# The second half of v begins with tokens 1024 to 1535, read from tiles still on chip; loads of heads and gate are spread over more units

## The chip, the cores and the metric

The kernel runs on one core of one Trainium2 chip. The metric is the time of one execution on the device, in microseconds; for the kernel before it is the median of three runs. A profile is one further execution of the same program, taken with the hardware profiler, and has a time of its own.

## The reference

Two attention blocks of 32 heads work on the same x (2048 tokens, 1024 columns): A is linear attention, B is softmax attention, and a gate g, one number per token, mixes their outputs.

```python
x = A_x                                              # 1 x 2048 x 1024, fp32
g = _sigmoid((x * gate_w).sum(-1, keepdims=True))
# A: q, k, v = x @ A_wqkv; phi(t) = where(t > 0, t + 1, exp(t)) + 1e-6
#    kv = phi(k)^T v, z = sum(phi(k)); o = phi(q) kv / (phi(q) z + 1e-6); a = o @ A_wo
# B: q, k, v = x @ B_wqkv; p = softmax(q k^T * Dh ** -0.5); o = p v; b = o @ B_wo
return g * a + (1 - g) * b
```

## The kernel before

fp32 products are made of three fp32r products: each operand is split into a high and a low part, and `three` (lines 148 to 157) issues high by high, high by low and low by high into one PSUM bank. A matmul has a stationary part of 128x128 and a moving part of 128x512.

**Opening (lines 526 to 671).** x stands on chip as tiles of the program's `big` set, in two passes: J = 0 holds tokens 0 to 1023, J = 1 tokens 1024 to 2047. In a pass, `X11`, `X21`, `X12`, `X22` hold the split x: `X` with row l + 1 and column jj + 1 holds the k-blocks k with k % 2 = l and the 512 tokens 2J + jj. Each piece is a pair of `big` tiles, high and low. `PLACE` (line 307) says which: for J = 1 it puts X11 in (4, 5), T4 (and X12) in (8, 9), X21 in (10, 11), X22 in (12, 13), T1 in (0, 1), T2 in (2, 3), T3 in (6, 7). `v_pass` makes the first 512 columns of v of block B; then sixteen `quad`s make q and k of B by a Strassen-like scheme of seven products each, in the order X11, X21, X22, T1, T2, T3, T4. The split x of all tokens is written to DRAM (`xs`) by `spill`. q and k go to DRAM as `qk`, v as `v`.

**The last quad** of J = 1 runs beside `leave()` (lines 674 to 688), one step of it between products: it splits the weights of the second half of v into `big` 16 to 19 and loads the first three halves of x for the next stage.

**The linear stage, `linear()` (line 926).** It runs over units. A unit is a kind, a chunk of columns and one tile of 128 tokens: first sixteen units "v" (the second 512 columns of v of block B, tokens 0 to 15 in order of tiles), then "kv", "q" and "o" for block A. A unit makes 24 matmuls, eight k-steps of three. Its stationary x comes from DRAM: `load_half(m)` (line 761) loads half m, that is four k-blocks of unit m // 2, high and low, 256 KB each, into `xh_t[m % 3]`, three buffers, two of them in `big` 4. The load of half m + 3 is issued right after the matmuls that read half m. In the sixteen "v" units other things are issued at fixed k-steps: `first`, fourteen loads of q, k and v of heads 0 and 1 (`load_q`, `load_k`, `load_v`, 64 KB per piece, 192 KB for the rest of a q), and the steps of `gate()` (line 487): each loads one tile of x (512 KB, two buffers) and has VectorE multiply the tile before it with the gate's weights and sum it (line 495). So the load of an x waits for the product that last read its buffer.

**Beside it.** `maxima()` makes the score products of a head (line 1123), and VectorE takes the maximum of each row (line 1128); during the "v" units a rule lets it begin after six units, with eight or nine products in each of the units after that. `rows(h)` turns the maxima (PE, line 1140) and writes them to `big` as `mh` and `ml`. From unit 16 on, `heads_()` makes the exponentials and the products with v. A planner (lines 1589 to 1693) puts the streams in order while the program is built, by modelled costs; what it issues is fixed then. PE executes its instructions in this order.

**Queues.** All loads and stores here go through `dma` (line 166) and are issued by the SP engine, in the program's order: an issue that has to wait for its buffer holds up all that stand behind it. The exception are the folds of the heads' sums, which POOL issues.

**The turn to kv.** In units 14 and 15 the weights of the kv units are loaded (`load_w`, line 715) and split by ACT and VectorE (lines 728 and 730) into the places of v's weights, as these come free.

In the "q" units, `queries` turns a result; a "q" unit waits until the one three units before it has been turned. `keys_alone(n)` issues what is left of the products of keys up to unit n.

Of the kernel before, what the change touches and what calls it, by code (L numbers as in the profile page):

```python
# [19 lines left out]
P = 128  # L20
# [27 lines left out]
def kernel(  # L48
# [23 lines left out]
    HK = NK // 2  # L72
    NT = S // P
# [230 lines left out]

    KH = NK // 2
    NPAIR = NJ // 2
    PLACE = [(4, 5), (8, 9), (10, 11), (12, 13), (0, 1), (2, 3), (6, 7)]
    PRODUCTS = ["X11", "X21", "X22", "T1", "T2", "T3", "T4"]
    PLACES = [dict(zip(PRODUCTS, PLACE)), dict(zip(["X11", "T4", "X21", "X22", "T1", "T2", "T3"], PLACE))]
    for side in PLACES:  # L310
# [22 lines left out]
    def xpiece(J, name, p, i):  # L333
        return side_x(J, name, p)[:, i * C:(i + 1) * C]

    def xname(jj, l):
        return "X%d%d" % (l + 1, jj + 1)
# [16 lines left out]
    def v_out(c, t, ps, va):  # L354
        nc.scalar.copy(va, ps)  # L355
        dma(v_d[c][:, t, :], va)
# [316 lines left out]

    def leave():

        load_half(0)
        load_half(1)
        split_v1(raw_a[2], 2)
        split_v1(raw_a[3], 3)
        yield  # L680
        xh_t[2] = sb.tile([P, 2 * HK * P], F32R, name="xh")
        load_half(2)
        split_v1(raw_a[0], 0)
        split_v1(raw_a[1], 1)
        yield
        for k in range(KH, NK):
            split_v1(raw_b[k - KH], k)
            yield
# [67 lines left out]
    def xstat_lin(n, k, p):  # L756

        o = (p * HK + k % HK) * P
        return xh_t[(2 * n + k // HK) % 3][:, o:o + P]

    def load_half(m):

        if m >= 2 * len(units):
            return
        i, t = units[m // 2]
        ks = slice(m % 2 * HK, (m % 2 + 1) * HK)
        for p, src in enumerate(oA_d if chunks[i][0] == "o" else xs):
            o = p * HK * P
            dma(f32(xh_t[m % 3][:, o:o + HK * P].rearrange("p (k c) -> p k c", c=P)), src[t][:, ks])
        xp_ready[m] = T["sp"] + 3.2  # L770
# [155 lines left out]
    def linear():  # L926
# [9 lines left out]
        for n, (i, t) in enumerate(units):  # L936
            kind, c = chunks[i]
            follow = chunks[i + 1] if i + 1 < len(chunks) else None
            lag = 2 if kind == "v" else 0

            def renew(k):

                mark = Later(None, 0.0, 0.0, 0, None)
                w_left[k][:] = [mark]
                next_w.append((follow, k, mark, nc.vector if kind == "v" else nc.gpsimd))
                pump_w(kind == "v")

            yield bank_at
            b = take()
            ps = bank[b]  # L950
            T["pe"] = max(T["pe"], free[b])
            lin_kind[0] = kind
            if (kind, c, t) in (("q", 1, 2), ("q", 1, 8), ("o", 0, 2), ("o", 0, 8)):
                load_mix()
            for k in range(NK):
                yield lambda: ended(w_left[k], w_ready[k], xp_ready.get(2 * n + k // HK, 0.0))
                need(w_left[k])
                stat = [xstat_lin(n, k, p) for p in range(2)]
                for m, _ in enumerate(three(ps, stat, (wpart(k, 0), wpart(k, 1)), k)):
                    lin_pe(1.0)  # L960
                    if m < 2:
                        yield always
                store_mix()
                if kind == "v":
                    if first and (k == 1 or k == 5 and t):
                        first.popleft()()
                    if t > TPC and k in (3, 7):
                        next(gates, None)
                if k % HK == HK - 1:
                    load_half(2 * n + k // HK + 3)  # L970
                if k == 0 and n + 7 == len(units) and not o_main[0]:
                    load_o(0)
                if k == 1 and n + 1 == len(units):
                    assert finished[0] >= H - 2
                    need(pr_left[extra_pr[2]])
                    xo_t[0] = big_tile(PR[extra_pr[2]], F32R)
                    split_o(0, slice(0, NK - 1))
                if k == NK // 2 and n + 1 == len(units) and over["head"]:
                    split_o(1, slice(0, NK - 1))
                if k == NK - 1:  # L980
                    yield from extra
                if follow and follow[0] == "o":
                    if t == NT - 1:
                        w_left[k].clear()
                        yield lambda: 0.0 if mixed.count((k // HK, follow[1])) == 8 * HK else None
                        load_wa(follow[1], k)
                    continue
                if follow and t == NT - 2 and k == 0:
                    yield lambda: None if mix_here or stores else 0.0
                if follow and t == NT - 2 and k < min(LEAD_W, NK):  # L990
                    coming_w.append(load_w(*follow, k, LEAD_W + 1))
                if follow and t == NT - 1 and k >= lag:
                    renew(k - lag)
            extra = iter(())
            e, r = mid[3 + n % 3], mid[6]
            if kind == "v":
                give(b, use("act", 0.5, T["pe"] + LATENCY["pe"]))
                v_out(c, t, ps, mid[11 - n % 2])
            elif kind == "kv":
                va = mid[7][:, (n % 2) * HC:(n % 2 + 1) * HC]  # L1000
                yield from keys_alone(n - 2)
                nc.scalar.copy(va, ps[:, HC:])
                use("act", 0.28, T["pe"] + LATENCY["pe"])
                end = phi(ps, e, HC)

                def more(end, c=c, t=t, e=e, ps=ps):
                    pk = e[:, :HC]
                    nc.vector.scalar_tensor_tensor(pk, pk, 1.0, ps[:, :HC], op0=ALU.min, op1=ALU.add)
                    z_end[c % 2] = use("pool", 0.69, end)
                    if t == 0:  # L1010
                        nc.gpsimd.tensor_copy(zsum[c % 2], pk)
                    else:
                        nc.gpsimd.tensor_add(zsum[c % 2], zsum[c % 2], pk)

                todo = [defer(more, end, 0.34)]
                give(b, 0.0, todo)
                keys(n, c, t, e, va, todo)
                if t == NT - 1:
                    extra = keysum(c)
            elif kind == "q":  # L1020
                yield lambda: None if n - 3 not in turned and chunks[units[n - 3][0]][0] == "q" else 0.0
                end = phi(ps, e, C)
                d = dn[n % 2]

                def sums(_, e=e, ps=ps):
                    nc.vector.scalar_tensor_tensor(ps, e, 1.0, ps, op0=ALU.min, op1=ALU.add)

                def scaled(_, c=c, ps=ps, r=r):
                    nc.vector.tensor_mul(r, ps, zrep[:, c * C:(c + 1) * C])

                last = []

                def dens(end, r=r, d=d, last=last):
                    nc.vector.tensor_reduce(d, r.rearrange("p (h d) -> p h d", d=DH), AX.X, ALU.add)
                    nc.scalar.add(d, d, eps)
                    last[0].at = use("act", 0.2, end)

                def divide(_, t=t, e=e, ps=ps, d=d):
                    nc.vector.reciprocal(d, d)
                    nc.vector.scalar_tensor_tensor(  # L1040
                        e.rearrange("p (h d) -> p h d", d=DH), ps.rearrange("p (h d) -> p h d", d=DH),
                        g_sb[:, t:t + 1], d.unsqueeze(2).to_broadcast([P, C // DH, DH]),
                        op0=ALU.mult, op1=ALU.mult)

                todo = chain(((sums, 0.63), (scaled, 0.63), (dens, 0.63), (divide, 0.9)), end)
                last.append(todo[-1])
                give(b, 0.0, todo)
                tasks.append((lambda todo=todo: None if kv_todo else both(ended(todo + o_left), o_free[(len(turned) + 1) % 2], bank_at()),
                              lambda n=n, c=c, t=t, e=e, todo=todo: queries(n, c, t, e, todo)))
            else:  # L1050
                res = mid[(7, 10)[n % 2]]
                give(b, use("act", 0.5, T["pe"] + LATENCY["pe"]))
                nc.scalar.copy(res, ps)
                dma(ra_d[t][:, c * C:(c + 1) * C], res)
            if follow and follow[0] != "o" and t == NT - 1:
                for k in range(NK - lag, NK):
                    renew(k)
# [661 lines left out]
```

## Time and profile before

| | us |
|---|---|
| median of three runs | 2843.2 |
| lowest, highest | 2840.29, 2846.19 |
| the profiled execution, its time | 2843.68 |
| its span, first to last instruction | 2841.9 |
| PE busy | 2823.3 |
| DVE busy | 2229.5 |
| POOL busy | 1909.1 |
| ACT busy | 1596.6 |

The span is what the profile covers; the time holds some 1.8 us more around it. In the profile an engine is named PE (matmuls), PEld (weight loads, beside PE), DVE (VectorE), ACT (ScalarE), POOL (GpSimd), SP (the queue of DMA issues). A timeline row gives the start, the duration, engine and line, the operation, and what was written from what; brackets give the idle time of the engine before it and what ended it. A windows row gives a stretch, its length, the busy time and instructions of each engine, the mean granted clock of PE, the share of the DMA engines that was busy, and GB/s. Matmuls overlap, and each row of one shows some 0.39 us, so the distance of two starts says more than a duration.

### The profile page before, as it was taken

Reading aid. Unit: us, or ns where it says so; the run is one execution under the profiler, and the core shown is the slowest. Engines: PE = TensorE matmul, PEld = TensorE weight load, DVE = VectorE, ACT = ScalarE, POOL = GpSimd, SP = SyncE. Lnnn points to the kernel's source line nnn. Section 1 sums busy time; section 2 is a strip of 40 time slices with the busy share of each in tenths; the row PEclk is TensorE's granted clock in tenths of the full one; section 3 lists DMA queues with packets and bytes.
Section 4 is the critical chain, followed back from the end, with each engine's and each line's share of the span. In section 5 each row is a group of like instructions: output and inputs, shape, how many; then the busy total and the mean of one; then the engine's idle time right before and its main releaser. Section 6 shows DMA issues by size and latency. Waiting matters only on the chain.

```text
span 2841.9 us, 46542 instructions
## 1 busy us (share of the span) xinstructions
PE 2823.3 (99%) x15944; PEld 2053.7 (72%) x15944; DVE 2229.5 (78%) x3659; ACT 1596.6 (56%) x2994; POOL 1909.1 (67%) x894
## 2 busy tenths in 40 slices
PE   9999999999999999999999999999999999999999
PEld 8888876676677766776677767777776766676787
DVE  7777747788888888888888888788878888887522
ACT  5334320566676666666666666566666656666400
POOL 0000010499999999999999999889889888885000
PEclk9999999999999999999999999999999999999999
DMA  8867669433344334333434344455666465544642
GB/s 274 252 221 231 215 217 309 156 100 100 97 131 108 98 93 127 94 103 102 127 98 107 95 129 138 149 175 170 196 185 178 133 162 141 153 114 128 203 147 78
DMA packets 376713, 428.56 MB, mean 151 GB/s; under 512 B 105006, under 2 KB 210734, under 8 KB 376476
## 3 DMA queue, kind: packets, MB, share of 16 engines
q1 hardware_dynamic: 362876, 412.47, 47.7%
q0 software_dynamic: 13600, 13.11, 3.4%
q8 instruction: 127, 2.08, 0.3%
q14 instruction: 110, 0.90, 0.1%
HBM read 298.06 MB, written 112.98 MB: 145 GB/s over the span
## 4 chain that ended last, share of the span: by engine, by line
PE 97%; DMA 2%; SPq 0%; ACT 0%; DVE 0%; issue 0%; ACTq 0%; DVEq 0%
PE bank L1297 17%; PE bank L1123 16%; PE bank L1454 16%; PE bank L152 15%; PE bank L155 15%; PE bank L157 15%; PE bank L1188 1%; DMA big<-xs 1%; PE bank L906 1%; PE bank L795 0%; DMA v<-mid 0%; DMA big<-qk 0%; DMA xh<-xs 0%; PE bank L1180 0%; DMA big<-in_x 0%; DMA big<-wa 0%
## 5 line engine op out<-in xcount | busy, mean ns | idle before, releaser
L1389 POOL TENSOR_TENSOR big<-big,big 128x512 f32<-128x512 f32 (+2 forms) x694 | 1644.2, 2373 | 116.4 <-ACT big L1300 73.6
L1128 DVE TENSOR_REDUCE mx<-bank 128x1 f32<-128x512 f32 x2048 | 1303.6, 683 | 252.0 <-PE bank L1123 247.8
L1300 ACT ACTIVATE big<-bank 128x512 f32<-128x512 f32 x2048 | 1179.2, 601 | 430.8 <-PE bank L1297 361.7
L1297 PE MATMUL bank<-big,big 128*128 128x512 f32 x1888 | 742.0, 394 | 0.3 <-ACT mid L355 0.3
L1123 PE MATMUL bank<-big,big 128*128 128x512 f32 x1888 | 739.9, 392 | 1.2 <-ACT big L1300 1.1
L152 PE MATMUL bank<-big,big 128*128 128x512 f32 x1600 | 626.3, 391 | 4.6 <-DMA big<-xs 4.4
L157 PE MATMUL bank<-big,big 128*128 128x512 f32 x1596 | 623.4, 391 | 2.3 <-DMA big<-xs 2.1
L155 PE MATMUL bank<-big,big 128*128 128x512 f32 x1600 | 624.3, 390 | 0.0
L1454 PE MATMUL bank<-big,mid 128*32 128x512 f32 x4096 | 454.1, 593 | 0.0
L1297 PEld LDWEIGHTS bank<-big,big 128*128 128x128 f32 x1888 | 354.0, 188 | 126.0 <-issue 46.9
L1123 PEld LDWEIGHTS bank<-big,big 128*128 128x128 f32 x1888 | 354.6, 188 | 77.5 <-ACT big L1300 4.6
L152 PEld LDWEIGHTS bank<-big,big 128*128 128x128 f32 x1600 | 300.9, 188 | 73.0 <-DMA big<-xs 6.4
L157 PEld LDWEIGHTS bank<-big,big 128*128 128x128 f32 x1596 | 299.9, 188 | 67.6 <-DMA big<-xs 5.2
L155 PEld LDWEIGHTS bank<-big,big 128*128 128x128 f32 x1600 | 300.9, 188 | 62.8 <-DVE big L294 0.2
L1454 PEld LDWEIGHTS bank<-big,mid 128*32 128x32 f32 x4096 | 142.6, 110 | 265.2 <-issue 265.2
L1080 POOL MEMSET big<- 32x512 f32 (+1 forms) x4 | 3.7, 950 | 386.3 <-PE bank L157 386.3
L1405 DVE TENSOR_TENSOR bank<-bank,big 128x512 f32<-128x512 f32 x364 | 251.6, 691 | 5.5 <-ACT big L1300 3.6
L152 PE MATMUL bank<-big,xh 128*128 128x512 f32 x384 | 151.2, 394 | 2.5 <-DMA xh<-xs 1.4
L157 PE MATMUL bank<-big,xh 128*128 128x512 f32 x384 | 150.9, 393 | 1.7 <-DMA xh<-xs 1.7
L155 PE MATMUL bank<-big,xh 128*128 128x512 f32 x384 | 150.4, 392 | 0.2 <-DMA big<-wa 0.2
L1385 POOL TENSOR_TENSOR big<-big,big 128x1536 f32<-128x1536 f32 (+1 forms) x31 | 122.3, 3946 | 35.7 <-ACT big L1300 31.8
L1463 ACT COPY mid<-bank 128x512 f32<-128x512 f32 x32 | 18.8, 588 | 207.2 <-PE bank L1454 200.4
(125 smaller groups left out, 1979.9 us busy)
## 6 DMA issues: line engine op xcount, KB each, us to landing
big<-xs SPq DMA_DIRECT2D x300, 256.0 KB
big<-qk SPq DMA_DIRECT2D x720, 64.0 KB
xh<-xs SPq DMA_DIRECT2D x148, 256.0 KB
qk<-mid SPq DMA_DIRECT2D x128, 256.0 KB
big<-oA SPq DMA_DIRECT2D x84, 256.0 KB
xs<-big SPq DMA_DIRECT2D x64, 256.0 KB
oA<-mid SPq DMA_DIRECT2D x64, 256.0 KB
big<-big POOLq DMA_DIRECT2D x50, 256.0 KB, 5.5
```

Of the source, the lines that this page charges most:

```text
L152: yield nc.tensor.matmul(ps, sh, mh_, start=(kt == 0), stop=False)
L155: yield nc.tensor.matmul(ps, sh, ml_, start=False, stop=(late and last))
L157: yield nc.tensor.matmul(ps, sl, mh_, start=False, stop=last)
L906: nc.tensor.transpose(pt[:, i * P:(i + 1) * P], pq[:, i * P:(i + 1) * P], ident)
L1123: nc.tensor.matmul(bank[b], q[:, t % TPC * P:(t % TPC + 1) * P], k[:, j * C:(j + 1) * C], start=True, stop=True)
L1128: nc.vector.tensor_reduce(m[:, t, j:j + 1], bank[b], AX.X, ALU.max)
L1297: nc.tensor.matmul(bank[b], k[:, t * P:(t + 1) * P], q_cols(h, j), start=True, stop=True)
L1300: nc.scalar.activation(pr_t[i][:, j * C:(j + 1) * C], bank[b], AF.Exp, scale=SCALE)
L1385: nc.gpsimd.tensor_add(lacc[:, :qp], pr(0)[:, :qp], pr(1)[:, :qp])
L1389: nc.gpsimd.tensor_add(lacc[:, sl], lacc[:, sl], pr(t)[:, sl])
L1405: nc.vector.tensor_add(lacc[:, qp:] if t == NT - 1 else l_b[:, :n], l_b[:, :n], src)
L1454: nc.tensor.matmul(av_b[j * DH:(j + 1) * DH, :], v[:, t, :], pr(t)[:, j * C:(j + 1) * C], start=(t == 0), stop=(t == NT - 1))
```

## The change

The places (4, 5) and (6, 7) of `PLACE` change their roles, so that X11 of J = 1 stands in (6, 7), beside the buffers of x in `big` 4. The "v" units take their tokens in another order: `token` turns t by half, so that units 0 to 3 make tokens 1024 to 1535, units 4 to 7 tokens 1536 to 2047, units 8 to 15 tokens 0 to 1023. Units 0 to 3 take their stationary x from X11 and X21 on chip (`n < TPC`, TPC is 4), and `load_half` does nothing for halves 0 to 7. `leave` loads no x; halves 8, 9 and 10, for unit 4 and the first part of unit 5, are issued in unit 1. `first` issues two loads in each of units 0 to 3 and then one per unit (before: one in unit 0, then two). The gate begins in unit 2 (before: unit 5), with one step in even units and two in odd ones (before: two in each). The "q" units get a call of `keys_alone(n - 3)`.

```diff
-    PLACE = [(4, 5), (8, 9), (10, 11), (12, 13), (0, 1), (2, 3), (6, 7)]
+    PLACE = [(6, 7), (8, 9), (10, 11), (12, 13), (0, 1), (2, 3), (4, 5)]
...
     def leave():
 
-        load_half(0)
-        load_half(1)
         split_v1(raw_a[2], 2)
         split_v1(raw_a[3], 3)
         yield
         xh_t[2] = sb.tile([P, 2 * HK * P], F32R, name="xh")
-        load_half(2)
...
+    def token(i, t):
+        return (t + NT // 2) % NT if chunks[i][0] == "v" else t
+
     def load_half(m):
 
-        if m >= 2 * len(units):
+        if m >= 2 * len(units) or m < 2 * TPC:
             return
         i, t = units[m // 2]
+        t = token(i, t)
...
-                stat = [xstat_lin(n, k, p) for p in range(2)]
+                if n < TPC:
+                    stat = [xpiece(1, xname(0, k % 2), p, k // 2)[:, t * P:(t + 1) * P] for p in range(2)]
+                else:
+                    stat = [xstat_lin(n, k, p) for p in range(2)]
...
-                    if first and (k == 1 or k == 5 and t):
+                    if first and (k == 1 or k == 5 and n < TPC):
                         first.popleft()()
-                    if t > TPC and k in (3, 7):
+                    if t > 1 and (k == 3 or k == 7 and t % 2):
                         next(gates, None)
-                if k % HK == HK - 1:
+                if n == 1 and k == 0:
+                    for m in range(2 * TPC, 2 * TPC + 3):
+                        load_half(m)
+                if k % HK == HK - 1 and 2 * n + k // HK >= 2 * TPC:
                     load_half(2 * n + k // HK + 3)
...
-                v_out(c, t, ps, mid[11 - n % 2])
+                v_out(c, token(i, t), ps, mid[11 - n % 2])
...
             elif kind == "q":
+                yield from keys_alone(n - 3)
```

## The prediction

> **What bounds the kernel now.** I read the page first, then the windows around the second half of v, then PE's timeline and waits there, and last the SP and DVE rows that feed it.
>
> ```profile
> span 2841.9 us, 46542 instructions
> ...
> PE 2823.3 (99%) x15944; PEld 2053.7 (72%) x15944; DVE 2229.5 (78%) x3659; ACT 1596.6 (56%) x2994; POOL 1909.1 (67%) x894
> ```
>
> PE is busy all the time, and the change removes no matmul. It can only give back time that PE loses, so the question is where PE loses any. The windows are cut at unit starts: unit 0 of v's second half starts at 397.57, unit 1 at 403.01, unit 6 at 438.52, unit 9 at 469.15, unit 15 at 513.62, unit 16 (kv) at 522.05; 424.61 is the start of unit 4, 536.17 that of unit 17.
>
> ```profile
> core 0: us, PE busy (x) PEld busy (x) DVE busy (x) ACT busy (x) POOL busy (x), PEclk, DMA share, GB/s
> 397.57:403.01 5.44, 5.44 (x25) 4.50 (x24) 2.72 (x5) 1.38 (x3) 2.26 (x2) 1.00 0.53 193
> 403.01:424.61 21.60, 19.53 (x74) 14.18 (x72) 0.00 (x0) 1.76 (x3) 0.00 (x0) 0.92 0.92 254
> 424.61:438.52 13.91, 12.53 (x49) 8.47 (x48) 0.00 (x0) 1.17 (x2) 0.00 (x0) 1.00 0.90 257
> 438.52:469.15 30.63, 25.44 (x99) 18.87 (x98) 21.62 (x37) 1.76 (x3) 0.00 (x0) 0.94 1.01 321
> 469.15:513.62 44.47, 44.43 (x196) 36.27 (x195) 43.46 (x78) 4.00 (x8) 0.00 (x0) 1.00 0.83 283
> 513.62:522.05 8.43, 6.18 (x25) 4.19 (x24) 3.22 (x6) 3.69 (x6) 0.00 (x0) 1.00 0.90 261
> 522.05:536.17 14.12, 12.70 (x51) 9.22 (x51) 9.48 (x16) 8.35 (x17) 2.81 (x2) 1.00 0.62 207
> 536.17:2606.00 2069.83, 2069.32 (x12603) 1450.00 (x12602) 1763.95 (x2932) 1357.93 (x2576) 1894.81 (x879) 1.00 0.46 127
> ```
>
> The first row gives the unit of account: 24 matmuls in 5.44 us, 0.2267 each. An x counts instructions that reach over an edge too, so the weight loads (PEld) give the number of matmuls. Loss is length less matmuls times 0.2267: units 1 to 3, 21.60 - 72 x 0.2267 = 5.28; units 4 and 5, 13.91 - 48 x 0.2267 = 3.03; units 6 to 8, 30.63 - 98 x 0.2267 = 8.41; units 9 to 14, 0.26; unit 15, 2.99; unit 16, 14.12 - 50 x 0.2267 = 2.79 (one of the 51 is the next unit's). Units 1 to 8 lose 16.7 us, units 15 and 16 another 5.8, and the 2070 us after that lose 0.5. The stage is fed by DMA: share 0.9 and more up to unit 8.
>
> ```profile
> 406.38 0.50 PE L152 MATMUL bank<-big,big 128*128 128x512 f32 x1 [0.48 <-DMA big<-xs]
> ...
> 408.54 0.50 PE L157 MATMUL bank<-big,big 128*128 128x512 f32 x1 [1.43 <-DMA big<-xs]
> ...
> 409.67 0.63 PE L152 MATMUL bank<-big,big 128*128 128x512 f32 x1
> 410.10 0.63 PE L155 MATMUL bank<-big,big 128*128 128x512 f32 x1
> ...
> 431.61 0.50 PE L152 MATMUL bank<-big,big 128*128 128x512 f32 x1 [0.71 <-DMA big<-xs]
> ...
> 444.78 0.50 PE L152 MATMUL bank<-big,big 128*128 128x512 f32 x1 [2.25 <-DMA big<-xs]
> ...
> 462.44 0.50 PE L152 MATMUL bank<-big,xh 128*128 128x512 f32 x1 [1.15 <-DMA xh<-xs]
> ...
> 464.47 0.79 PE L157 MATMUL bank<-big,xh 128*128 128x512 f32 x1 [1.29 <-DMA xh<-xs]
> ```
>
> Every wait here is for a half unit of stationary x (big or xh from xs). After two of them the matmuls come 0.43 apart (409.67, 410.10): the granted clock is halved, which the PEclk column shows as 0.92 and 0.94. 0.08 of 21.60 us is 1.7, at half speed for 3.4 us, so each such stretch costs 1.7 us of progress.
>
> **The change, part by part.**
>
> *Units 0 to 3 from tiles on chip.* Sixteen loads of 256 KB go (10 of them inside the stage), and with them every wait of units 1 to 3: -5.28. Nothing else can hold these units: the weights are split as before, and unit 0, which needs all of them, ran its 24 matmuls in 5.44. The exchange of places 4,5 and 6,7 goes through every product alike, and costs nothing. The first loads for unit 4 are issued in unit 1 and have three units to land. Units then start at 397.57 + 5.44 n: unit 4 at 419.3, where before it started at 424.61.
>
> *Units 4 to 8.* The x buffer still holds three halves, so each later half is loaded only when the half three before it is done, two halves (5.44 us without maxima) before its use. What a load takes, and what holds it in SP's queue:
>
> ```profile
> 401.60 1.34 SPq L169 DMA_DIRECT2D big<-qk  x3
> 403.04 1.79 SPq L169 DMA_DIRECT2D big<-xs  x4
> ...
> 437.41 0.42 SPq L169 DMA_DIRECT2D big<-in_x  x1
> ...
> 454.14 3.92 SPq L169 DMA_DIRECT2D big<-in_x  x1
> 458.15 0.86 SPq L169 DMA_DIRECT2D xh<-xs  x2
> ```
>
> ```profile
> 444.09 1.23 DVE L495 SCALAR_TENSOR_TENSOR big<-big,zrep 128x1024 f32<-128x1024 f32 x1 [42.93 <-DMA big<-in_x]
> ...
> 445.24 2.48 DVE L1128 TENSOR_REDUCE mx<-bank 128x1 f32<-128x512 f32 x4
> ...
> 456.37 1.23 DVE L495 SCALAR_TENSOR_TENSOR big<-big,zrep 128x1024 f32<-128x1024 f32 x1 [0.76 <-DMA big<-in_x]
> ```
>
> ```profile
> 423.57 4.74 DMA big<-xs
> ...
> 458.62 5.80 DMA xh<-xs
> ```
>
> The last two rows, of the chain, show a half's load landing 4.7 to 5.8 us after its issue, and SP issues its two parts in 0.86: 5.6 to 6.7 against 5.44. The gate's x is slower: issued at 437.41, read by DVE at 444.09, 6.7 us. It has two buffers, so the third x waits on SP for DVE's product of the first. At 454.14 SP stood 3.92 us for that, until the product at 456.37 was through; the x half behind it left at 458.15, and PE paid at 462.44 and 464.47.
>
> In the changed order the gate starts in unit 2, and SP has x number 3 ahead of the half for unit 5's second part. That x follows DVE's product of x number 1, issued at the middle of unit 3, 416.6. It lands 4.7 (the fastest row above) to 6.7 us later, at 421.3 to 423.3; with DVE's 1.23, SP is free at 422.5 to 424.5, and the place is due at 422.05 (419.33 + 2.72, half of unit 4). With 0.42 for x and 0.86 for the pair, and 4.7 to 5.8 to land (counted from the pair's second part), the half is there at 428.5 to 431.5. PE wants it at 419.33 + 5.44 + 2.72 = 427.5: a stall of 1 to 4 us. I take 3.0, because SP issues 13 transfers in unit 1 and the gate's weights and two x close behind, so the queue is as full as in the 6.7 us row. Behind it, the half for unit 6's second part leaves after three q pieces and an x; with 17 matmuls per half from there it has 6.6 us instead of 5.44, against up to 6.7 plus the 0.42 of x: 0 to 2, and I take 1.5, since the q pieces are the long ones. From unit 6 on a half takes 16 or 17 matmuls (3.6 us), two give 7.3, and the gate brings 1.5 x per unit instead of 2: 0.
>
> *The clock.* Both halvings followed waits that sum to 1.9 to 2.4 us within 3.5; a single wait of 2.25 (444.78) brought none. A stall of 3 us is longer than all of these, so I charge one halving, 1.7 (0 to 3.4).
> The Trainium skill ("TensorE: Matmul & The Clock Gate", "What's actually happening") has the clock fall after an idle window of about 3.4 us. The rows differ, it fell after gaps of 1.43 and 1.29 us; by the page the sum would be 1.7 us better, and I go by the rows.
>
> Residue of units 4 to 8: 3.0 + 1.5 + 1.7 = 6.2, in place of 3.03 + 8.41 = 11.44.
>
> *Heads' loads spread, gate spread.* The same transfers, on the same queue, up to unit 9 instead of 7. K and q of head 0 are there before unit 6, where maxima begin as before; head 1's come before its twelve maxima of units 13 and 14. DVE hides the gate: five of 16 products now come before the first reduce, and 1.5 x 1.23 + 8.5 x 0.62 = 7.1 us per unit stand against 7.4 on PE. Were DVE late, PE would wait for a bank; in 469.15 to 513.62 DVE had 43.46 of 44.47 us and PE lost 0.26. Charged 0.
>
> *Token order, units 15 and 16, the queries' new line.* Stores go to other rows, at the same size. From unit 13 the order on PE differs by a few places until unit 21, and is the same from there. The rows of the row maxima move:
>
> ```profile
> 505.62 1.09 SPq L169 DMA_DIRECT2D big<-xs  x2
> 507.05 0.32 SPq L169 DMA_DIRECT2D v<-mid  x1
> 507.42 0.91 SPq L169 DMA_DIRECT2D mid<-in_a_wqkv  x2
> 508.43 1.69 SPq L169 DMA_DIRECT2D big<-mh  x2
> 510.22 1.41 SPq L169 DMA_DIRECT2D big<-ml  x2
> ```
>
> They now stand ahead of the x pair for unit 15's first half, 3.1 us of issue that can cost it 0 to 3 us, and no longer ahead of its second half and of four of kv's five first weights, whose late arrival makes part of the 5.8 us. These answer each other: 0, from -3 to +3. The queries' line adds a wait only while a key product is open; PE's order past unit 21 being the same, it acts on nothing: 0.
>
> **Sum.** -5.28 - (11.44 - 6.2) + 0 = -10.5 us. The profiled execution took 2843.68 us for its span of 2841.9; its time would be 2833.2. It stands 0.5 over the median of the runs, 2843.2, which gives **2832.7 us**.
>
> **The rivals.**
> *The waits only move.* The queue is as full as before in units 4 to 8, these keep their 11.44, and only 5.28 is won: 2837.9. For it: shares of 0.90 to 1.01 there. Against it: 10 of the stage's loads are gone and the gate's x are drawn out.
> *No SP block.* Units 0 to 3 leave the queue so empty that x number 1 lands in 4.7 us; 3.0 becomes 1.0, the clock stays, 0.5 is left behind it: 1.5, a gain of 15.2, 2828.0. Against it: unit 1 issues six x loads and seven others at once.
> *Slower: x of the gate ahead of the halves on SP.* Each block like that at 454.14 costs 1.15 + 1.29 + 1.7 = 4.1 us. Units 4 to 14 must lose 16.7 + 5.7 = 22.4 before the kernel is 0.2% slower: six such blocks among the 13 later x. It decides once DVE's work per unit passes PE's, so that products lag and each x waits for its buffer; the 7.1 against 7.4 speaks against it. Six give 2843.2 - 16.7 + 24.6 = 2851.1.
> *It does not do what it says.* The tiles on chip cannot be late, the product before unit 0 reads them; but the six loads for unit 4, now issued only in unit 1, could land after 419.33 + 5.28 = 424.6, and all that units 1 to 3 gave is lost there, with the queue behind it as before: 2843.2. From 404 that would be 20 us for what took 4.7 to 6.7.
>
> **How the numbers follow.** A measurement of this kernel tells 0.2%, 5.7 us, from no change (the runs before lie between 2840.29 and 2846.19). Forecast 0.48, moved waits 0.26, no block 0.19, slower 0.04, nothing done 0.03. Faster: 0.48 + 0.19 + 0.11 (the better two fifths of the moved waits) = 0.78; same: 0.15 + 0.03 = 0.18; slower 0.04. The range goes from a gain of 16.7 (all of units 1 to 8), 2826.5, to one of 3.2 (all waits moved, units 15 and 16 two worse), 2840; it leaves out about 0.19.
>
> **What would show it.** Right: no PE wait for xs before unit 5; unit 4 at 419.3; a wait of 1 to 4 us at unit 5's second half, with an SP row of an x load of a microsecond or more just before; DMA share under 0.95 from unit 6; at most one half-clock stretch; 5 to 7 us lost in units 15 and 16; nothing new after 540. Wrong: a wait in units 0 to 4, SP rows of x over 2 us again and again, DVE full with PE waiting for a bank, or lost time in units 15 and 16 above 9.

## The result, and the profile after

| us | before | after |
|---|---|---|
| median (lowest to highest) of 15 runs each | 2842.2 (2839.74 to 2846.19) | 2837.73 (2835.99 to 2840.15) |
| the profiled execution, its time | 2843.68 | 2839.65 |
| its span | 2841.9 | 2837.8 |

The ratio is 0.9984, its interval 0.9976 to 0.9992: 4.5 us, or 0.16%, faster. The time lies in the range of the prediction, 5 us above its number, and almost on that of the rival in which the waits only move (2837.9). By the prediction's own measure, 0.2%, it is no change.

The page of the kernel after, its head and the line of busy times. PE has as many instructions as before; the busy times say little, since what PE lost sits in one stage. The windows show it.

```profile
span 2837.8 us, 46516 instructions
...
PE 2818.0 (99%) x15944; PEld 2053.8 (72%) x15944; DVE 2231.0 (79%) x3659; ACT 1597.9 (56%) x2994; POOL 1910.0 (67%) x894
```

Windows of the kernel after, with the columns of the windows of before. In this execution unit 0 starts at 398.51, unit 1 at 403.95, unit 4 at 420.27 and unit 5 at 425.71; the third row is the one long gap:

```profile
402.90:419.00 16.10, 16.10 (x73) 13.33 (x72) 0.00 (x0) 1.77 (x3) 0.00 (x0) 1.00 0.83 246
419.00:428.43 9.43, 9.43 (x43) 7.61 (x41) 1.23 (x2) 1.18 (x2) 0.00 (x0) 1.00 0.98 249
428.43:436.50 8.07, 0.16 (x1) 0.00 (x0) 3.05 (x5) 0.00 (x0) 0.00 (x0) 0.70 0.98 311
436.50:443.00 6.50, 6.50 (x18) 5.09 (x19) 0.66 (x2) 0.59 (x1) 0.00 (x0) 0.58 1.04 316
...
402.90:470.00 67.10, 59.19 (x251) 48.39 (x250) 30.69 (x51) 5.29 (x9) 0.00 (x0) 0.92 0.92 283
500.00:545.00 45.00, 40.99 (x176) 32.39 (x176) 34.44 (x58) 26.05 (x49) 16.96 (x7) 1.00 0.53 168
545.00:2600.00 2055.00, 2053.62 (x12531) 1435.97 (x12530) 1747.69 (x2905) 1343.79 (x2547) 1881.46 (x874) 1.00 0.46 127
```

Units 1 to 4 and the first half of unit 5 lose nothing: in the first two rows PE is busy all the time at full clock. All that is lost up to 470 is 67.10 - 250 x 0.2267 = 10.4, where before units 1 to 8 lost 16.7. It is lost at one place: in the third row PE stands for 8 us with the DMA engines 0.98 busy, and in the fourth it runs at a granted clock of 0.58. PE's timeline of the kernel after, around that gap, with three later rows:

```profile
428.20 0.39 PE L157 MATMUL bank<-big,big 128*128 128x512 f32 x1
436.50 0.79 PE L152 MATMUL bank<-big,xh 128*128 128x512 f32 x1 [7.91 <-DMA xh<-xs]
437.09 0.63 PE L155 MATMUL bank<-big,xh 128*128 128x512 f32 x1
437.52 0.63 PE L157 MATMUL bank<-big,xh 128*128 128x512 f32 x1
...
441.79 0.45 PE L152 MATMUL bank<-big,big 128*128 128x512 f32 x1
...
513.87 0.50 PE L152 MATMUL bank<-big,big 128*128 128x512 f32 x1 [2.07 <-DMA big<-xs]
...
524.02 0.50 PE L1131 MATMUL bank<-big,big 128*128 128x512 f32 x1 [1.35 <-ACT big L1308]
```

This is the second half of x of unit 5. The twelve matmuls behind it are 0.43 apart instead of 0.2267: 2.4 us on top of 7.9. Why the half came so late stands in the chain of waits of the kernel after (start, length, what; SPq is SP's queue of issues):

```profile
405.75 4.71 DMA xh<-xs
...
410.47 6.66 DMA big<-qk
...
417.14 0.35 SPq L169
...
419.88 0.60 SPq L169
...
420.52 7.92 DMA big<-in_x
428.53 1.25 DVE big L495 x2
429.80 0.36 SPq L169
...
430.26 6.20 DMA xh<-xs
436.50 0.79 PE bank L152
```

It is read from below. The half left SP at 430.26 and took 6.20 to land. Ahead of it in SP's order stood an x of the gate (429.80), which waited for VectorE's product (428.53), which waited for an x issued at 420.52. Two more steps matter. At 417.14 SP issued the gate's weights, into a buffer of their own, and yet the chain ties this issue to a load of q and k sent at 410.47. The program explains it: in both kernels the loads and stores of SP count their ends on eight semaphores in turn, so each waits until the eighth before it has landed, and at most eight are in flight. And SP was late altogether, as its rows show:

```profile
402.53 2.71 SPq L169 DMA_DIRECT2D big<-qk  x6
...
419.88 0.60 SPq L169 DMA_DIRECT2D mid<-v  x1
420.52 4.57 SPq L169 DMA_DIRECT2D big<-in_x  x1
425.13 1.36 SPq L169 DMA_DIRECT2D big<-qk  x3
...
427.48 1.55 SPq L169 DMA_DIRECT2D big<-qk  x3
429.80 0.36 SPq L169 DMA_DIRECT2D big<-in_x  x1
430.26 0.85 SPq L169 DMA_DIRECT2D xh<-xs  x2
```

The wait for VectorE's product cost SP little: its row at 427.48 ends at 429.03, and the x left at 429.80, 0.77 us later. From 402.53 to the half there are 40 issues in 27.7 us, 0.69 us each, among them the loads of the heads in units 0 to 4. With eight places that is one transfer in 5.5 us per place, about the time that the transfers of the chain took to land (4.71 to 7.92). The half could leave once PE is through the middle of unit 4. By its own clock that is 422.99, 5.44 ahead of the end of unit 5's first half at 428.43; SP reaches it 7.3 us late.

### The profile page after: what moved, and what is told of

Same layout as the page of the kernel before. It is cut to its first block, busy times and chain, and to the rows that moved or that the text cites. A ratio compares the mean times of both kernels' runs of the same rounds, so it can differ in the third digit from the quotient of the medians.

```text
span 2837.8 us, 46516 instructions
## 1 busy us (share of the span) xinstructions
PE 2818.0 (99%) x15944; PEld 2053.8 (72%) x15944; DVE 2231.0 (79%) x3659; ACT 1597.9 (56%) x2994; POOL 1910.0 (67%) x894
## 4 chain that ended last, share of the span: by engine, by line
PE 97%; DMA 2%; SPq 0%; DVE 0%; issue 0%; ACT 0%; ACTq 0%; DVEq 0%
PE bank L1305 17%; PE bank L1131 16%; PE bank L1462 16%; PE bank L152 15%; PE bank L155 15%; PE bank L157 15%; PE bank L1196 1%; PE bank L907 1%; PE bank L796 0%; DMA xh<-xs 0%; PE bank L1188 0%; SPq L169 0%; DMA big<-in_x 0%; DMA big<-qk 0%; DMA extra<-in_xT 0%
## 5 line engine op out<-in xcount | busy, mean ns | idle before, releaser
L152 PE MATMUL bank<-big,xh 128*128 128x512 f32 x376 | 148.9, 396 | 8.2 <-DMA xh<-xs 7.9
L155 PE MATMUL bank<-big,xh 128*128 128x512 f32 x376 | 148.2, 394 | 0.2 <-DMA big<-wa 0.2
L157 PE MATMUL bank<-big,xh 128*128 128x512 f32 x376 | 147.8, 393 | 0.0
```

The lines of the kernel that those rows point to most:

```text
L152: yield nc.tensor.matmul(ps, sh, mh_, start=(kt == 0), stop=False)
L155: yield nc.tensor.matmul(ps, sh, ml_, start=False, stop=(late and last))
L157: yield nc.tensor.matmul(ps, sl, mh_, start=False, stop=last)
```

## The experiments

Four causes were set against one another. G: the gate's x, waiting for VectorE, holds the half on SP. V: the gather of v (`load_v`, 2048 pieces of 128 B), behind which an issue takes 4 us. S: the eight in flight on SP. B: the DMA engines are full, and what is not urgent goes first. The profiled executions are up to 1.6 us apart ahead of the stage already (the 1701st matmul stands at 387.60 before, 388.54 after, 387.26 in thin_gate, 388.85 in slow_from4), so waits are compared, and the lateness of the half against the middle of unit 4 of the same execution, and not times of day. Every kernel ran beside the kernel before, whose median there was 2842.2 to 2843.6.

| kernel | median (lowest to highest), runs | ratio to before, interval |
|---|---|---|
| half_first | 2842.49 (2840.14 to 2843.93), 11 | 1.0002, 0.9993 to 1.0011 |
| v_last | 2839.69 (2835.77 to 2842.07), 11 | 0.9992, 0.9983 to 1.0001 |
| on_chip_only | 2835.22 (2833.49 to 2837.57), 11 | 0.9978, 0.9969 to 0.9987 |
| spread_only | 2842.69 (2841.56 to 2846.12), 11 | 1.0005, 0.9996 to 1.0014 |
| pool_heads | 2835.90 (2834.12 to 2837.51), 10 | 0.9978, 0.9969 to 0.9987 |
| pool_gate | 2839.92 (2836.84 to 2843.09), 11 | 0.9989, 0.9981 to 0.9998 |
| pool_both | 2834.43 (2832.25 to 2837.22), 7 | 0.9973, 0.9962 to 0.9984 |
| split_loads | 2840.02 (2836.26 to 2840.84), 11 | 0.9991, 0.9982 to 0.9999 |
| thin_gate | 2833.91 (2831.69 to 2838.36), 6 | 0.9969, 0.9957 to 0.9981 |
| heads_slow | 2832.61 (2831.78 to 2836.74), 5 | 0.9963, 0.9950 to 0.9975 |
| slow_late | 2833.93 (2833.46 to 2835.63), 5 | 0.9966, 0.9954 to 0.9979 |
| slow_from4 | 2832.45 (2829.77 to 2832.96), 5 | 0.9957, 0.9945 to 0.9970 |

**The half ahead of the gate's step.** In the kernel after, the order of two statements is exchanged.

```diff
-                    if t > 1 and (k == 3 or k == 7 and t % 2):
-                        next(gates, None)
...
                 if k % HK == HK - 1 and 2 * n + k // HK >= 2 * TPC:
                     load_half(2 * n + k // HK + 3)
+                if kind == "v" and t > 1 and (k == 3 or k == 7 and t % 2):
+                    next(gates, None)
```

> The changed kernel, with one edit: in each v unit the load of the next half of x is issued ahead of the gate's step instead of behind it. Theory G (the gate's x, which waits for VectorE's product two x earlier, holds the half on SP): the wait of 8.07 us at unit 5's second half falls by 3 us or more, and the time by as much against the changed kernel. Theory V (SP lost its time upstream, at the DMA that follows the gather of head 0's v, whose SP row took 4.57 us) and theory S (SP may have eight DMAs in flight, so 40 DMAs ahead of this half take 27 us whatever their size): SP was idle only 0.77 us before that x and took 0.42 for it, so the half leaves 1.2 us earlier, the wait is 6.5 to 7.2, and the time falls by 1 to 2.

SP and PE of this kernel, timeline rows:

```profile
427.18 0.83 SPq L169 DMA_DIRECT2D xh<-xs  x2
...
432.27 0.79 PE L152 MATMUL bank<-big,xh 128*128 128x512 f32 x1 [4.52 <-DMA xh<-xs]
```

What PE waited for from 397 to 545 in this kernel (us in total, times, longest):

```profile
PE bank L152 <- DMA xh<-xs: 4.5, 1, 4.5
PE bank L1131 <- DVE mx L1136: 4.1, 5, 1.2
```

The half is 5.0 us late instead of 7.3, and the wait falls from 7.91 to 4.52. So an x ahead of the half does cost time at this place, but not all of the 3.4 us is G's: after stood 0.77 us for VectorE and 0.46 for that x, while the gate's weights, which leave before the edit acts, left 0.9 us earlier against PE here, and the half landed in 5.1 us instead of 6.2. The other 4.5 us are there without an x ahead, since SP is 5 us late by itself. But the kernel becomes 4.8 us slower than after: the x now come later, their products fall among the reductions of the maxima, and PE waits for VectorE (mx) five times, 4.1 us in all, where after has no such wait. What was won at unit 5 is paid there; the profiled execution (2840.14) was the fastest of its runs and only 0.5 us slower than that of after, so where the rest of the 4.8 us goes is not shown.

**The gather last.** The two gathers of v go behind the other loads of the heads.

```diff
-            first.append(lambda h=h: load_v(h))
+        first.extend(lambda h=h: load_v(h) for h in range(2))
```

> The changed kernel, with one edit: the gathers of v for heads 0 and 1 come last among the fourteen loads of heads, so in unit 3 a q of head 1 (three DMAs) takes the place of the gather. Theory V: the DMA behind no longer takes 4.57 us on SP, the first x of the gate land earlier, the half for unit 5 leaves 2.5 to 4.5 us earlier, the wait falls from 8.07 to 3.5 to 5.5, and the time falls by 2.5 to 5. Theory S: two DMAs more stand ahead, so the half leaves no earlier, or up to 1.4 us later; the wait is 8 to 9.5 and the time the same or 1 us longer. Theory G: no change as long as the x of the gate stand where they are.

SP and PE of this kernel:

```profile
423.56 0.35 SPq L169 DMA_DIRECT2D big<-in_x  x1
...
429.43 1.11 SPq L169 DMA_DIRECT2D xh<-xs  x2
...
436.91 0.79 PE L152 MATMUL bank<-big,xh 128*128 128x512 f32 x1 [9.55 <-DMA xh<-xs]
```

The issue of 4.57 is gone (0.35), and the wait grew to 9.55: V alone falls. The three pieces of q that took the gather's place cost as much: SP waited among them for earlier transfers to land, and the x left only at 423.56. With three issues in the place of one, this is no clean trial of the gather's price.

**Each part alone.** on_chip_only is the kernel after with the conditions of before; spread_only is the kernel before with the conditions of after (the same lines, reversed).

```diff
-                    if first and (k == 1 or k == 5 and n < TPC):
+                    if first and (k == 1 or k == 5 and t):
                         first.popleft()()
-                    if t > 1 and (k == 3 or k == 7 and t % 2):
+                    if t > TPC and k in (3, 7):
                         next(gates, None)
```

> The changed kernel with the loads of heads and the gate at their units of before (one load of heads in unit 0, then two per unit; the gate from unit 5 on, two steps per unit): the on-chip tiles and the token order alone. 32 DMAs instead of 40 stand ahead of unit 5's half. Theory S: 8 x 0.69 = 5.5 us earlier, a wait of 2 to 3.5 there. Theory G: no x of the gate stands ahead, a wait under 2. Theory V: the gather, now in the second half of unit 3, still stands ahead, a wait of 3 to 6. Then the gate, beginning in unit 5 with two steps per unit, brings back 3 to 6 us in units 6 to 8. In all 2 to 7 us below the changed kernel if the spreading is what costs, the same or longer if it pays.

> The kernel before with the loads of heads and the gate spread as in the change, and nothing else: all units load their x. Theory S: eight loads of heads and six DMAs of the gate join the sixteen loads of x in units 0 to 3, and every one takes one of eight places, so units 1 to 4 lose 5 to 12 us more than before and units 6 to 8 win back 3 to 6: 0 to 8 us longer than the kernel before. If the spreading helps by itself, by theory of the prediction (fewer x per unit of the gate), it is 3 to 6 us shorter.

SP and PE of on_chip_only:

```profile
422.65 0.84 SPq L169 DMA_DIRECT2D xh<-xs  x2
...
437.29 0.79 PE L152 MATMUL bank<-big,big 128*128 128x512 f32 x1 [3.06 <-DMA big<-xs]
```

Without the gate's five loads and with one load of the heads less ahead of it, 32 issues instead of 40, the half leaves 0.6 us after the middle of unit 4, and unit 5 waits for nothing. One wait of 3.06 is left at unit 6's second half. The on-chip tiles alone gain 7.0 us; the spreading takes 2.5 of them back by the medians, though the intervals of the two kernels overlap, and the row of SP is the better witness. On the kernel before the spreading changes nothing that can be measured.

**Another queue.** `dma` gets a second queue; pool_heads sends the loads of the heads by POOL, pool_gate the gate's, pool_both both.

```diff
+    by_pool = [False]
+
     def dma(to, of):
 
         T["sp"] = max(T["sp"], T["pe"]) + DMA_ISSUE
-        nc.sync.dma_start(to, of)
+        (nc.gpsimd if by_pool[0] else nc.sync).dma_start(to, of)
```

The calls that are to go by POOL run with `by_pool` set.

> The changed kernel with the fourteen loads of heads (40 DMAs with the gathers) issued by POOL, which is idle in this stage, instead of SP. Same bytes, same DMA engines. Theory S (eight SP DMAs in flight; every DMA waits for the eighth before it): 25 of the 40 DMAs ahead of unit 5's half leave SP's queue, the half leaves at its place, at 422 to 424, the wait of 8 us there is gone or under 1.5, no half clock, and the time is 6 to 10 us below the changed kernel's 2837.7. Theory V alone (the gather): the same at unit 5, if smaller: a wait of 3 to 5. If the DMA engines themselves were the bound (bytes), the wait stays at 5 or more and the time falls by less than 3.

> The changed kernel with the gate's loads (weights and sixteen x) issued by POOL instead of SP; the loads of heads stay on SP. Theory G (the x, waiting for VectorE, hold the halves): the wait at unit 5 is gone, the time 6 to 10 us below the changed kernel. Theory S: five DMAs fewer ahead, 5 x 0.69 = 3.5 us, and no hold of 0.77: the wait falls from 8 to 3 to 5, and the time by 3 to 6. Theory V: the gather's 4.57 us falls on the q behind it: the wait falls by 1 to 4.

> Both sets of loads by POOL: SP keeps the x halves and the stores of v alone. By theory S the waits of units 1 to 8 are gone but for 0 to 2 us, and the time is 8 to 12 us below the changed kernel, 2826 to 2830. If POOL's gate loads, each waiting for VectorE, hold the loads of head 1 behind them, the maxima of unit 14 wait, and it is no better than the heads alone.

PE waits 6.6, 9.0 and 4.0 us at unit 5 in the three. One row of each chain of waits says why, first pool_heads:

```profile
415.05 11.63 DMA big<-in_x
```

then pool_gate:

```profile
417.61 9.52 DMA v<-mid
```

then pool_both:

```profile
410.05 13.87 DMA v<-mid
425.04 7.33 DMA xh<-xs
```

A window of pool_heads shows how full the engines are ahead of the gap, where after has 0.83 in the same stretch:

```profile
397.00:428.00 31.00, 30.59 (x135) 24.98 (x134) 5.67 (x10) 4.70 (x8) 21.79 (x35) 1.00 0.97 286
```

With two queues more transfers are in flight at once, and each takes longer. In pool_heads the load of x number 1 (counted from 0) takes 11.6 us in place of 7.9, and x number 3, ahead of the half, waits for its product. A store of 256 KB takes 9.5 and 13.9; the four stores of after in this stretch landed in 2.2 to 5.9. In pool_gate SP's eighth issue behind that store had to wait for it. In pool_both the store of unit 1 held the buffer that ACT's copy of unit 3 needed (424.01), and with it that unit's store on SP (424.62) and the half behind it, though neither a head's nor the gate's load was in SP's queue. So S alone falls, and B shows: the engines are full, and the transfers share them. pool_gate has no x of the gate on SP and waits longest, so G alone falls too; it isn't a clean trial of G, since POOL sends the x earlier. By the medians pool_heads gains 1.8 and pool_both 3.3 us over after, and pool_gate loses 2.2; the intervals of all three overlap with that of after.

**Number and bytes.** split_loads cuts the six loads issued in unit 1 into twelve of half the size; thin_gate loads and multiplies only the first 512 columns of x and of the gate's weights, so the gate sums half of its products.

```diff
-            dma(f32(xh_t[m % 3][:, o:o + HK * P].rearrange("p (k c) -> p k c", c=P)), src[t][:, ks])
+            for r in (slice(0, P // 2), slice(P // 2, P)) if m < 2 * TPC + 3 else (slice(0, P),):
+                dma(f32(xh_t[m % 3][r, o:o + HK * P].rearrange("p (k c) -> p k c", c=P)), src[t][r, ks])
```

```diff
-            dma(xn[t % 2], x[t * P:(t + 1) * P, :])
+            dma(xn[t % 2][:, :C], x[t * P:(t + 1) * P, :C])
```

> The changed kernel with the six loads for units 4 and 5 cut into two of 64 partitions each: six DMAs more on SP, not a byte more. Theory S: up to 6 x 0.69 = 4 us later for all that follows on SP, less what smaller DMAs land sooner: the wait at unit 5 rises from 8 to between 9.5 and 12.5, the time by 1 to 5. Theories G and V, and a bound by bytes: no change, the wait 7 to 9.

> The changed kernel with the gate's weights and x cut to their first 512 columns, so the gate sums half of each token's products: the same DMAs in the same places, 4.5 MB less of the gate's 8.9. Theory B (the 16 DMA engines are full from unit 2 to unit 6, and what the gate moves there is ahead of the half that PE waits for): two thirds of 5 x 1.5 us are ahead of that half, so the wait of 8 us at unit 5 falls to 3 to 5.5 and the time by 3 to 7. Theory S (the number of SP's DMAs alone, whatever their size): the wait stays at 6.5 to 9 and the time within 2 of the changed kernel.

SP and PE of split_loads:

```profile
421.03 6.30 SPq L169 DMA_DIRECT2D big<-in_x  x1
...
433.15 0.85 SPq L169 DMA_DIRECT2D xh<-xs  x2
...
438.19 0.79 PE L152 MATMUL bank<-big,xh 128*128 128x512 f32 x1 [10.55 <-DMA xh<-xs]
```

SP and PE of thin_gate:

```profile
419.72 2.97 SPq L169 DMA_DIRECT2D big<-in_x  x1
...
427.21 0.87 SPq L169 DMA_DIRECT2D xh<-xs  x2
...
432.21 0.80 PE L152 MATMUL bank<-big,xh 128*128 128x512 f32 x1 [4.90 <-DMA xh<-xs]
```

Both count. Six more issues of the same bytes make the half 11.1 us late instead of 7.3, and the wait 2.6 us longer (the medians differ by 2.3); the same issues with less to carry make it 5.5 us late, and the wait 3.0 shorter (3.8 by the medians). thin_gate's VectorE products are shorter as well, so not all of its gain is bytes. Both medians differ from that of after with intervals that overlap. A good part of both differences stands in one row, the x right behind the gather: its issue took 6.30 us in split_loads, 4.57 in after and 2.97 in thin_gate. So the gather's price is not fixed; it changed with edits that leave the gather as it is.

**Loads of the heads, one per unit.** Three kernels take one per unit from the start; they differ in the gate. heads_slow has the gate as after, slow_late as before, slow_from4 from unit 4 on (the second pair of lines).

```diff
-                    if first and (k == 1 or k == 5 and n < TPC):
+                    if first and k == 1:
...
-                    if t > 1 and (k == 3 or k == 7 and t % 2):
+                    if t > 3 and (k == 3 or k == 7 and t % 2):
```

> The changed kernel with one load of heads in every unit instead of two in units 0 to 3: the gate as in the change. Eleven or twelve DMAs and the gather fewer ahead of unit 5's half. Theories S and B: the half leaves near its place, the wait falls from 8 to 0 to 3, the time by 4 to 8 against the changed kernel. Theory G (the gate's x alone): the wait stays above 5.

> One load of heads in every unit, and the gate as before the change (from unit 5, two steps per unit), with the on-chip tiles: nothing of the gate and only half the loads of heads ahead of unit 5's half. Theory B: no wait at unit 5; the gate's start at unit 5 then meets only one load of heads, so the 3.4 us that the on-chip tiles alone still lost at unit 6 shrink to 0 to 2, and the time is 2830 to 2834, below the on-chip tiles alone (2835.2). If the gate's two x per unit are the limit there, it is 2834 to 2836.

> One load of heads in every unit and the gate with one and a half steps per unit from unit 4 on, with the on-chip tiles. Theory B: the traffic is flattest here, waits in units 1 to 8 of 0 to 3 us in all, time 2828 to 2833. Against it: the gate ends only in unit 15, and if its last products or its exponential hold the turn of the row maxima or the weights of kv, units 14 to 16 lose up to 5 us more: 2833 to 2838.

SP and PE of heads_slow:

```profile
416.35 4.88 SPq L169 DMA_DIRECT2D big<-in_x  x2
...
423.71 0.85 SPq L169 DMA_DIRECT2D xh<-xs  x2
...
429.46 0.50 PE L152 MATMUL bank<-big,xh 128*128 128x512 f32 x1 [2.04 <-DMA xh<-xs]
```

and three windows of slow_from4:

```profile
397.00:428.00 31.00, 31.00 (x138) 25.68 (x137) 4.54 (x8) 4.70 (x8) 4.02 (x3) 1.00 0.68 208
428.00:440.00 12.00, 10.28 (x37) 7.69 (x37) 5.60 (x9) 0.59 (x1) 0.00 (x0) 0.86 1.02 352
440.00:500.00 60.00, 60.00 (x267) 49.57 (x266) 55.41 (x94) 4.96 (x9) 0.00 (x0) 1.00 0.92 302
```

Of all edits this single condition does the most: in heads_slow five loads of the heads in place of nine stand ahead of the half, it is 1.9 us late in place of 7.3, the wait is 2.0 in place of 7.9, and the kernel is 5.1 us faster than after, with intervals that do not overlap. The gather is one of the four loads that no longer stand there, so this run does not part V from S and B. What is left of the wait is G: in the row at 416.35 x number 2 waits for VectorE's product of x number 0, and SP stands 4.1 us for it (416.77 to 420.88). In slow_from4 the DMA share up to 428 falls to 0.68, and from 440 to 500 PE has no idle time. It is 0.43% faster than before (0.30 to 0.55%), and than after by 5.3 us. The three lie within 1.5 us and, with five runs each, cannot be told apart; where the gate starts makes no difference that shows, once the heads are out of the way.

## Why the prediction was right, and where it was off

The time lies in the range, and units 0 to 3, 15 and 16 came out as worked out. But less than half of the gain came, 4.5 us of 10.5, and the range held it by its width: it reached down to a gain of 3.2, at which all waits of units 4 to 8 only move. The outcome that came, no change by the measure of 0.2%, had a chance of 0.18, faster one of 0.78.

*Units 0 to 3 from tiles on chip, -5.28:* right. No wait for xs before unit 5, units 1 to 3 lose nothing, and the tiles were never late. The six loads for units 4 and 5 were in time. Unit 4 starts at 420.27, the 419.3 that were foretold and the 0.9 us by which this execution runs later.

*The stall at unit 5's second half, 3.0 (1 to 4):* this is the step that failed. It was placed at the right half, and x number 3 does stand ahead of that half and wait for VectorE's product of x number 1. But SP stood only 0.77 us for it, and the sign that was named, an SP row of an x of a microsecond or more just before, is not there (0.36 at 429.80): SP itself was late, for which the sum has no term. It shows first in the first time of the sum. This let x number 1 leave at 416.6, the middle of unit 3 by PE's clock. By the clock of this execution that place is at 417.5, and SP sent it at 420.52, because its queue was already 3 us late; the issue took 4.57, VectorE read the x at 428.53 in place of 422.2 to 424.2 (421.3 to 423.3 and the 0.9 by which this execution runs later), and the stall became 7.91. The prediction priced SP as if only waits for buffers delayed it. The transfers ahead entered only into the time that a load takes to land; in SP's own time the loads of the heads and the stores were not counted, neither as issues (0.69 us each, 40 of them) nor as bytes. heads_slow shows it: with four loads of heads fewer, the gather among them, the rest unchanged, the stall is 2.0, and that rest is the mechanism of the prediction, an x that holds SP until VectorE has read an earlier one. How SP's lateness shares out among the number of issues, their bytes and the gather stays open.

*The row at 454.14 of before:* misread. Its 3.92 us were put down to an x that waits for VectorE; in SP's rows it follows the gather of v, as do the 4.57 at 420.52 after. The row ahead of it in before:

```profile
453.47 0.57 SPq L169 DMA_DIRECT2D mid<-v  x1
```

The x of after that did wait for VectorE has a row of 0.36 (429.80), since the wait stands ahead of the row. v_last removes that long issue and gains nothing, so the price of such a block was not a thing that could be carried over.

*Unit 6's second half, 1.5 (0 to 2):* no wait there; the lower bound. PE came to it so late that the load had landed.

*The clock, 1.7 (0 to 3.4):* a stretch of 10.24 us instead of one of 3.41, but 4.8 us of it lay in the wait itself, so that it cost 2.4. The sum for units 4 to 8, 6.2, was measured at 10.4: 4.2 short. The Trainium skill ("TensorE: Matmul & The Clock Gate", "What's actually happening") ties the fall of the clock to an idle window of about 3.4 us. This trace agrees (a wait of 7.91), but does not tell its rule from that of the rows; by the page, too, this stretch was to come.

*Spreading of heads and gate, 0:* wrong in itself, and the other face of the same error. It was looked at for what reads the loads (heads in time, VectorE not overfull: both came true), not for what stands behind them on SP. Beside the on-chip tiles it costs about 2.5 us (on_chip_only).

*Token order, units 15 and 16, 0 (-3 to +3):* right; from 500 to 545 after loses 45.00 - 176 x 0.2267 = 5.1, inside the 5 to 7 that were foretold.

*Nothing new after 540:* not quite. In the last window PE is idle 1.38 us of 2055, and before 0.51 of 2070; and from the first product of the exponentials with v to the last matmul the trace has 2286.0 before and 2287.9 after. Over all profiled executions this stretch goes from 2285.5 (spread_only) to 2288.8 (heads_slow), so it may be spread between executions; the cause stays open. With a start 0.9 us later in this execution, these account for the 6.5 us between the 2833.2 predicted for a profiled execution and 2839.65: 4.2 + 1.9 + 0.9, less some 0.5 from unit 9 to 16.

*The rivals.* "The waits only move" has the number, for another reason than it gave: not that units 4 to 8 keep their waits, but that the many became one, which with the slow clock behind it costs 10.3 us. The slower rival, x of the gate ahead of the halves, is at work at unit 5, once and not six times, and for 0.77 us.

## What to carry to other kernels

Loads that are not urgent are not free because their readers have time: on a queue that issues in order, what each costs is paid by the next urgent transfer behind it. Another queue helped less here (1.8 and 3.3 us by the medians) than fewer loads ahead (5.1): the DMA engines were full, and each transfer took longer. Before a load is moved forward, count the issues and bytes between now and the next urgent transfer, and take the time at which the queue reaches a place, not the time at which the reader does. If an early stage has been freed of loads, spread the others thinner into it (one per unit here); filling it up again gave back 2.5 of the 7.0 us that were won.

## What the runs showed of the hardware

The granted clock was halved in stretches of 3.41, 6.83 and 10.24 us, one, two and three times the same length: 10.24 with the wait of 7.91 (after) and 9.55 (v_last), 6.83 with 3.06 (on_chip_only) and 6.59 (pool_heads), and 3.41 with 4.52 (half_first), so the length doesn't follow from the wait alone. In all fourteen traces the stretches at full clock that end in a halved one are whole multiples of the same 3.413 us as well (in before the one between its two halvings has 51.20 us, 15 times; in after the one ahead of its halving has 426.67, 125 times). So the clock changed only on a grid of that length, whose points do not move with the waits, and how a wait lies on it is in part luck. How much idle time between two points brings a halving is not settled: 1.80 us did in before (406.01 to 409.42), 1.78 us in after (510.17 to 513.58) did not. After begins its stretch at 431.7, 3.1 us into the wait; so a long wait pays a good part of its slow time while it stands.

The time of a transfer depended on what else was in flight more than on its size: 4.7 us for a half of x at 405.75, 6.20 at 430.26, 7.33 in pool_both; and a store of 256 KB took 13.87 at its worst.
